# State products as 64 by 64 quarters, mask and decay tables by scans on chip, plan with later landings

## The chip, the cores and the metric

The kernel runs on one core of a Trainium2 chip. The metric is device time in microseconds (us), the median of several executions. TensorE is called PE here, VectorE DVE, ScalarE ACT, GpSimd POOL and SyncE SP; SP issues nearly all DMAs.

## What is computed

The reference is a linear attention with a decay for each of 8 heads, followed by two token-wise two-layer networks. Cut to what matters:

```python
# q, k, v: (2, 8, 768, 64); lam: 8 rates in 0.97 .. 0.99
Dmask = where(rel >= 0, lam ** rel, 0)                     # inside a block
intra = ((q_block @ k_block.T) * Dmask) @ v_block
inter = (q_block * lam ** (pos + 1)) @ kv_state            # what came before the block
kv_state = lam ** block * kv_state + (k_block * lam ** (block - 1 - pos)).T @ v_block
x = (intra + inter)                                        # 1536 tokens of 512 features
h = x @ w_in; x = (h * tanh(softplus(h))) @ w_out           # 512 -> 2048 -> 512
out = (relu(x @ w2_in) ** 2) @ w2_out
```

The kernel takes blocks ("chunks") of 128 positions, which gives the same result: 6 chunks in each of the 2 sequences, 12 in all.

## The kernel before

**Tiling.** A chunk `c` arrives as two tiles of 512 KB: `qk` (queries and keys, the 64 features of an even head on partitions 0 to 63, of the odd head on 64 to 127, four head pairs side by side) and `kv` (keys and values by position). `attention(j)` treats two chunks. For each chunk PE makes the scores `sc` (L392, 8 products), DVE multiplies them with `mask` into `a` (L271), PE multiplies `a` with the values into `xo` (L433, 8 products) and adds the state's part (L437, 8 products into the same bank). POOL scales the keys by the mask's last column (L398) and the queries by the decays `pw` (L403). PE makes the update `sd` of the state (L415), ACT or POOL scales the old state (L451, L447) and DVE adds the update (L271, or L462 for a sequence's first). The attention's output goes out of PSUM as `xh` (rounded) and `xl` (the rest), which the first network's `up` products read; its later tokens as `xr`.

**The state** is kept as 128 by 128 for each head pair, with the two heads' 64 by 64 blocks on the diagonal and zeros off it. Thus L437 contracts over 128 partitions, half of which are zeros, into 64 output columns. POOL zeroes the tile at L421; DVE adds each update in two instructions, one per head (64 partitions each).

**Tables.** The rates `lam` come by a tiny DMA on the ACT queue; seven DVE instructions (L324) double up the powers in eight rows; SP writes them to DRAM (`tab_d`, L338) and reads them back twice as `mask` (L344: row p starts p places earlier, 256 KB each) and twice as decays (L351).

**Weights** come as 64-bit numbers in tiles `st` of 512 KB; ACT and DVE make `m`, `t` and then the rounded `wh` and the rest `wl`. The networks' products are `up`, `p`, `b`, `e` and `dn`, all of 512 columns in three roundings (L278).

**Order.** `Plan` puts every operation in a list with an assumed length, and `plan.run(14.0, UNITS)` walks an assumed clock and picks, on each engine, the due operation whose inputs are ready. The order so found is fixed: engines then run their lists in order and wait on semaphores. `FIRST` fixes the order of SP's first DMAs, `LAG` is what is assumed between an operation's end and its effect. Ten products on zeros (L307) stand at the head of PE's list.

Of the kernel before, what the change touches and what calls it, by code (L numbers as in the profile page):

```python
# [20 lines left out]
P = 128  # L21
H = 8
# [35 lines left out]
class Plan:  # L58
# [7 lines left out]

    LAG = {"PE": 0.35, "DVE": 0.2, "ACT": 0.3, "POOL": 0.25, "SP": 2.2}

# [148 lines left out]
def attention_mlps(ctx, tc, lam, qk, kv, w_in, w_out, w2_in, w2_out, out):  # L217
# [19 lines left out]
    banks = ctx.enter_context(tc.tile_pool(name="banks", bufs=1, space=PSUM))  # L237
    dram = ctx.enter_context(tc.tile_pool(name="dram", bufs=1, space=bass.MemoryType.DRAM))
# [52 lines left out]

    W = 2 * CH
    tab_d = dram.tile([H, W], F32, name="tab_d")
    misc = Val("misc")
# [4 lines left out]

    def tab():  # L300
        return tl(misc, 4, W)[0:H, 2]

    def warm_up():

        z = zeros()
        for _ in range(WARM):
            nc.tensor.matmul(out=tl(warm)[:, 0], lhsT=z[:, 0:P], rhs=z, start=True, stop=True)  # L307

    warm = Val("warm", "P")
    zval = Val("zero", dtype=BF16)  # L310
    misc_parts = [(misc, "pw"), (misc, "tab")]

# [20 lines left out]

    op("ACT", 0.1, lambda: nc.scalar.dma_start(out=tab()[:, CH : CH + 1], in_=lam), [], [(misc, "lam")],
       name="lam", lag=2.2, due=0.0)
    op("DVE", 0.4, ones, [], [(misc, "tab")], name="ones")
    op("DVE", 1.2, powers, [(misc, "lam")], [(misc, "tab")], name="powers")
    op("SP", 0.1, lambda: nc.sync.dma_start(out=tab_d, in_=tab()), [(misc, "tab")], [("tab_d", 0)],  # L338
       name="tab_d", lag=2.2, due=FIRST["tab_d"])

    def masks():
        for e in range(2):

            nc.sync.dma_start(  # L344
                out=tl(mask, 2, NP, CH)[:, e],
                in_=bass.AP(tab_d.tensor, tab_d.offset + e * W, [[1, P], [2 * W, NP], [1, CH]]),
            )

    def decays():
        for e in range(2):  # L350
            nc.sync.dma_start(  # L351
                out=pw()[e * D : (e + 1) * D],
                in_=bass.AP(tab_d.tensor, tab_d.offset + e * W + CH, [[0, D], [2 * W, NP], [1, CH]]),
            )

    op("SP", 1.6, masks, [("tab_d", 0)], [(mask, 0)], name="masks", due=FIRST["masks"])
    op("SP", 0.9, decays, [("tab_d", 0)], [(misc, "pw")], name="decays", due=FIRST["decays"])


# [8 lines left out]
    def attention(j):  # L368
# [14 lines left out]
        for n, c in enumerate(cs):  # L383
            q, k, a = qks[n], kvs[n], avs[n]
            sc = Val(f"sc{c}", "P")

            def scores(sc=sc, q=q):
                t, o = tl(q, 2, NP, CH), tl(sc, 2, NP, CH)
                for p in range(NP):
                    for e in range(2):  # L390
                        r = slice(e * D, (e + 1) * D)
                        nc.tensor.matmul(out=o[:, e, p], lhsT=t[r, 1, p], rhs=t[r, 0, p], start=True, stop=True)  # L392

            op("PE", 0.95, scores, [(q, "q"), (q, "k")], [(sc, 0)], name=sc.name, rank=rank + n)
            op("DVE", 1.3, lambda a=a, sc=sc: tt(tl(a, 2, NP, CH), tl(sc, 2, NP, CH), tl(mask, 2, NP, CH), ALU.mult),
               [(sc, 0), (mask, 0)], [(a, 0)], name=a.name)
            if not (last and n):
                op("POOL", 1.3, lambda k=k: nc.gpsimd.tensor_tensor(  # L398
                    out=tl(k, NP, 4, D)[:, :, 1:3], in0=tl(k, NP, 4, D)[:, :, 1:3],
                    in1=tl(mask, 2, NP, CH)[:, :, :, CH - 1 : CH].rearrange("p e n o -> p n e o").to_broadcast(  # L400
                        [P, NP, 2, D]), op=ALU.mult), [(k, "k"), (mask, 0)], [(k, "k")], name=f"kd{c}")
            if not first or n:
                op("POOL", 1.35, lambda q=q: nc.gpsimd.tensor_tensor(  # L403
                    out=tl(q, 2, NP, CH)[:, 0], in0=tl(q, 2, NP, CH)[:, 0], in1=pw(), op=ALU.mult),
                   [(q, "q"), (misc, "pw")], [(q, "q")], name=f"qd{c}")
        sd, xo = Val(f"sd{j}", "P"), Val(f"xo{j}", "P")
# [12 lines left out]
        if first:  # L419
            state[s] = Val(f"state{s}")  # L420
            op("POOL", 1.1, lambda v=state[s]: nc.gpsimd.memset(tl(v), 0.0), [], halves(state[s]), name="state0")  # L421
        sv = state[s]
        for n, c in enumerate(cs):
            fresh = first and n == 0

            def outs(k=kvs[n], a=avs[n], q=qks[n], n=n, fresh=fresh, sv=sv):
                v, w, qd = tl(k, NP, 4, D), tl(a, 2, NP, CH), tl(q, 2, NP, CH)[:, 0]

                z, o = tl(sv, 2, NP, P)[:, n], tl(xo, NP, 2, CH)
                for p in range(NP):  # L430
                    for e in range(2):

                        nc.tensor.matmul(out=o[e * D : (e + 1) * D, p, n], lhsT=v[:, p, 0 if e else 3],  # L433
                                         rhs=w[:, e, p], start=True, stop=fresh)
                    for e in range(0 if fresh else 2):
                        r = slice(e * D, (e + 1) * D)
                        nc.tensor.matmul(out=o[r, p, n], lhsT=z[:, p, r], rhs=qd[:, p], start=False, stop=True)  # L437

            op("PE", 0.95 if fresh else 1.9, outs,
               [(kvs[n], "v"), (avs[n], 0)] + ([] if fresh else [(qks[n], "q"), (sv, n)]),  # L440
               [(xo, n)], name=f"xo{c}", rank=rank + 20 + n)
            if last and n:
                continue
            def scale(sv=sv, n=n):
                z, last = tl(sv, 2, NP, P), pw()[:, :, CH - 1 : CH]
                if t:
                    nc.gpsimd.tensor_tensor(  # L447
                        out=z[:, 1 - n], in0=z[:, n], in1=last.to_broadcast([P, NP, P]), op=ALU.mult)
                    return
# [3 lines left out]
            if not fresh:  # L453
                op("POOL" if t else "ACT", 1.3 if t else 1.2, scale, [(sv, n), (misc, "pw")], [(sv, 1 - n)],
                   name=f"ss{c}")

            def add(sv=sv, n=n, fresh=fresh):
                z, d = tl(sv, 2, NP, P)[:, 1 - n], tl(sd, 2, 2, NP, D)[:, 0, n]
                for e in range(2):
                    r = slice(e * D, (e + 1) * D)  # L460
                    if fresh:
                        nc.vector.tensor_copy(out=z[r, :, r], in_=d[r])  # L462
                    else:
                        tt(z[r, :, r], d[r], z[r, :, r], ALU.add)

            op("DVE", 0.9, add, [(sd, n), (sv, 1 - n)], [(sv, 1 - n)], name=f"sa{c}")
        cols = slice(i * 2 * CH, (i + 1) * 2 * CH)
        for p in range(2):
            if single(0, t):
                if i == 0:  # L470
                    x_hi[0, t, p], x_lo[0, t, p] = Val(f"xh{t}{p}", dtype=F32R), Val(f"xl{t}{p}", dtype=F32R)
                hi, lo = x_hi[0, t, p], x_lo[0, t, p]
                op("ACT", 0.65, lambda hi=hi, p=p: copy(tl(hi)[:, :, cols], tl(xo, 2, 2, 2 * CH)[:, p]),
                   [(xo, 0), (xo, 1)], [(hi, i)], name=hi.name)
                op("DVE", 0.75, lambda hi=hi, lo=lo, p=p: tt(
                    tl(lo)[:, :, cols], tl(xo, 2, 2, 2 * CH)[:, p], tl(hi)[:, :, cols].bitcast(F32), ALU.subtract),
                   [(xo, 0), (xo, 1), (hi, i)], [(lo, i)], name=lo.name)
            else:
# [9 lines left out]
    def weights(L, g, kind, kk):  # L488
# [4 lines left out]
        for i in range(2):  # L493
# [389 lines left out]
```

## Time and profile before

| | us |
|---|---|
| median of 3 runs (566.04 to 567.22) | 567.0 |
| the profiled execution: span from the first to the last instruction | 564.7 |
| PE busy in it | 549.6 |
| DVE, ACT, POOL busy | 307.6, 333.2, 33.1 |

The profiled execution has no time of its own beside its span. The median lies 2.3 us above that span; the difference is what surrounds the first and the last instruction, and it is taken as the same for both kernels. PE is busy in 97% of the span, so the time is PE's work plus the stretches at the start in which PE waits.

### The profile page before, as it was taken

The numbers are of one execution on the slowest core, as the hardware profiler recorded it, in microseconds if no ns is written. First come the engines' busy times: TensorE is split into PE (matmuls) and PEld (weight loads), VectorE is DVE, ScalarE is ACT, GpSimd is POOL, SyncE is SP. The second block draws the span as 40 slices with busy tenths as digits, with TensorE's granted clock in tenths as the row PEclk, the third lists the DMA queues.
The fourth block names the chain that finished last, engine by engine and source line by source line (L and its number), as shares of the span: only waits on it lengthen the run. The fifth ranks groups of instructions, "written<-read, shape, count | busy, mean of one in ns | idle before, by whom it ended". The sixth has DMA issues, their size and how long they took to land.

```text
span 564.7 us, 7047 instructions
## 1 busy us (share of the span) xinstructions
PE 549.6 (97%) x2934; PEld 454.9 (81%) x2934; DVE 307.6 (54%) x339; ACT 333.2 (59%) x374; POOL 33.1 (6%) x31
## 2 busy tenths in 40 slices
PE   3989999999999999999999999999999999999997
PEld 1878888888888888888888888888888888888885
DVE  2876985951453833582688865434363635743301
ACT  1435364643764566545886877347964789546920
POOL 1654600000000000000000000000000000000000
PEclk9899999999999999999999999999999999999999
DMA  8999000222141106041400401311222112300022
GB/s 238 409 409 339 6 2 0 75 74 74 38 149 38 38 2 203 21 122 65 149 1 0 150 0 38 111 39 37 76 74 75 60 48 79 113 0 1 18 95 111
DMA packets 15998, 50.52 MB, mean 89 GB/s; under 512 B 1624, under 2 KB 3168, under 8 KB 15968
## 3 DMA queue, kind: packets, MB, share of 16 engines
q1 hardware_dynamic: 15952, 50.08, 25.5%
q8 instruction: 23, 0.38, 0.3%
q14 instruction: 7, 0.06, 0.0%
q10 hardware_dynamic: 16, 0.00, 0.0%
HBM read 46.92 MB, written 3.15 MB: 89 GB/s over the span
## 4 chain that ended last, share of the span: by engine, by line
PE 96%; DMA 2%; DVE 1%; issue 0%; SPq 0%; DVEq 0%
PE dn L278 46%; PE up L278 20%; PE p L278 13%; PE e L278 7%; PE b L278 3%; PE xo L433 2%; PE sc L392 2%; PE xo L437 1%; DMA mask<-tab_d 1%; PE sd L415 1%; DVE t L510 0%; DMA tab_d<-misc 0%; DVE state L271 0%; DVE misc L324 0%; DMA misc<-in_lam_dram 0%
## 5 line engine op out<-in xcount | busy, mean ns | idle before, releaser
L515 DVE SCALAR_TENSOR_TENSOR t<-m,t 128x1024 int32<-128x1024 int32 x64 | 78.5, 1231 | 63.5 <-ACT m L507 61.4
L268 ACT ACTIVATE ac<-dn 128x1024 f32<-128x1024 f32 x46 | 47.3, 1029 | 101.9 <-PE dn L278 101.9
L271 DVE TENSOR_TENSOR gl<-h,gh 128x1024 fp32r<-128x1024 f32 x48 | 58.7, 1227 | 78.0 <-ACT gh L268 77.6
L278 PE MATMUL dn<-gh,wl 128*128 128x512 f32 x192 | 74.7, 389 | 0.0
L278 PE MATMUL dn<-wh,gh 128*128 128x512 f32 x192 | 74.7, 389 | 0.0
L278 PE MATMUL dn<-wh,gl 128*128 128x512 f32 x192 | 74.7, 389 | 0.0
L278 PE MATMUL dn<-gh,wh 128*128 128x512 f32 x192 | 74.7, 389 | 0.0
L278 PE MATMUL dn<-wl,gh 128*128 128x512 f32 x192 | 74.7, 389 | 0.0
L278 PE MATMUL dn<-gl,wh 128*128 128x512 f32 x192 | 74.7, 389 | 0.0
L268 ACT ACTIVATE gh<-h 128x1024 fp32r<-128x1024 f32 x48 | 50.3, 1053 | 0.7
L507 ACT ACTIVATE m<-st 128x512 f32<-128x512 f32 x64 | 40.1, 664 | 10.5 <-DMA st<-in_moe_w_in_dram 6.8
L271 DVE TENSOR_TENSOR wl<-t,wh 128x1024 fp32r<-128x1024 f32 x32 | 39.6, 1246 | 12.1 <-ACT wh L268 12.1
L606 ACT ACTIVATE h<-up 128x1024 f32<-128x1024 f32 x20 | 20.6, 1029 | 38.2 <-PE up L278 32.5
L268 ACT ACTIVATE wh<-t 128x1024 fp32r<-128x1024 f32 x32 | 33.4, 1052 | 15.3 <-DVE t L515 15.2
L278 PEld LDWEIGHTS dn<-gh,wl 128*128 128x128 f32 x192 | 36.0, 188 | 7.5
L278 PEld LDWEIGHTS dn<-wh,gh 128*128 128x128 f32 x192 | 36.0, 188 | 7.5
L278 PEld LDWEIGHTS dn<-gl,wh 128*128 128x128 f32 x192 | 36.0, 188 | 7.5
L278 PEld LDWEIGHTS dn<-wl,gh 128*128 128x128 f32 x192 | 36.0, 188 | 7.5
L278 PEld LDWEIGHTS dn<-wh,gl 128*128 128x128 f32 x192 | 36.0, 188 | 7.4
L278 PEld LDWEIGHTS dn<-gh,wh 128*128 128x128 f32 x192 | 36.0, 188 | 7.4
L268 ACT ACTIVATE dn<-ac 128x1024 f32<-128x1024 f32 x34 | 34.4, 1019 | 0.2
L510 DVE TENSOR_SCALAR t<-st 128x512 int32<-128x512 int32 x64 | 26.8, 446 | 7.0 <-DMA st<-in_moe_w_in_dram 5.7
(102 smaller groups left out, 987.3 us busy)
## 6 DMA issues: line engine op xcount, KB each, us to landing
st<-in_moe_w_in_dram SPq DMA_DIRECT2D x32, 512.0 KB, 4.7
st<-in_moe_w_out_dram SPq DMA_DIRECT2D x32, 512.0 KB, 3.6
qk<-in_qk_dram SPq DMA_DIRECT2D x12, 512.0 KB, 10.6
kv<-in_kv_dram SPq DMA_DIRECT2D x12, 512.0 KB, 10.4
out_dram<-ac SPq DMA_DIRECT2D x4, 512.0 KB, 2.8
out_dram<-ac SPq DMA_DIRECT2D x4, 256.0 KB, 2.0
mask<-tab_d SPq DMA_DIRECT2D x2, 256.0 KB, 6.3
misc<-tab_d SPq DMA_DIRECT2D x2, 128.0 KB, 6.8
```

What stands on the lines that cost most here:

```text
L268: nc.scalar.activation(out=o, in_=i, func=AF.Copy)
L271: nc.vector.tensor_tensor(out=o, in0=a, in1=b, op=alu)
L278: nc.tensor.matmul(out=out_, lhsT=a, rhs=b, start=first and i == 0 and not onto, stop=last and i == 2, skip_group_check=onto)
L392: nc.tensor.matmul(out=o[:, e, p], lhsT=t[r, 1, p], rhs=t[r, 0, p], start=True, stop=True)
L415: nc.tensor.matmul(out=o[e * D : (e + 1) * D, p], lhsT=t[:, p, 1 + e], rhs=t[:, p, 0 if e else 3], start=True, stop=True)
L433: nc.tensor.matmul(out=o[e * D : (e + 1) * D, p, n], lhsT=v[:, p, 0 if e else 3], rhs=w[:, e, p], start=True, stop=fresh)
L437: nc.tensor.matmul(out=o[r, p, n], lhsT=z[:, p, r], rhs=qd[:, p], start=False, stop=True)
L507: op("ACT", 0.67, lambda st=st, i=i: nc.scalar.activation(out=tl(m)[:, i], in_=tl(st, TB, 2)[:, :, 1].bitcast(F32), func=AF.Copy, scale=RA ...
L510: op("DVE", 0.5, lambda st=st, i=i: nc.vector.tensor_scalar(out=tl(t)[:, i], in0=tl(st, TB, 2)[:, :, 0], scalar1=29, scalar2=None, op0=ALU ...
L515: nc.vector.scalar_tensor_tensor(out=tl(t), in0=tl(m).bitcast(I32), scalar=scalar, in1=tl(t), op0=shift, op1=ALU.bitwise_or)
L606: op("ACT", 1.05, lambda: nc.scalar.activation(out=tl(h), in_=tl(src), func=AF.Relu if L else AF.Mish), halves(src), [(h, 0)], name=h.name)
```

## The change

1. **State free of zeros.** The state of a head pair is 128 by 64 (`tl(sv, 4, NP, D)`): the even head on partitions 0 to 63, the odd head on 64 to 127. The state's products are split from `outs` into `carried`: each contracts over 64 partitions into 64 columns, and four in a row take the four quarters of the array. For head pairs 2 and 3 the two heads change places in the output (`weighted`), and the tiles of the first network's `w_in` that meet them are loaded in two halves that change places too. The POOL memsets go; the scaling has half the elements; the addition is one DVE instruction instead of two, and for a sequence's first chunk an ACT copy.
2. **Tables on chip.** `tab_d`, its DMAs and the doubling go. `lam` is fetched as one row, PE spreads it over the partitions by three products of one row (`spread`, after three of the ten warm-up products), DVE copies that to SBUF, POOL writes an identity (`diagonal`), and DVE makes the eight masks and the four decays by one scan each.
3. **Plan.** SP's first DMAs are `qk0 kv0 st00000 ...`, the lag of SP's DMAs is 3.8 instead of 2.2, and the walk starts its due times at 6.0 instead of 14.0.

```diff
-    LAG = {"PE": 0.35, "DVE": 0.2, "ACT": 0.3, "POOL": 0.25, "SP": 2.2}
+    LAG = {"PE": 0.35, "DVE": 0.2, "ACT": 0.3, "POOL": 0.25, "SP": 3.8}
...
-        "st00000 qk0 tab_d kv0 st00001 masks decays qk1 kv1 qk2 kv2 qk3 kv3 st00010 st00011".split())}
+        "qk0 kv0 st00000 qk1 kv1 st00001 qk2 kv2 qk3 kv3 st00010 st00011".split())}
...
-    op("PE", 4.3, warm_up, [(zval, 0)], [(warm, 0)], name="warm", rank=-3000)
...
+    op("PE", 1.3, lambda: warm_up(3), [(zval, 0)], [(warm, 0)], name="warm", rank=-3000)
+
+    def spread():
+        o = tl(lamp)[:, 0]
+        nc.tensor.matmul(out=o[:, 0:H], lhsT=one(), rhs=row(), start=True, stop=True)
         for e in range(2):
...
+            nc.tensor.matmul(out=o[e * D : (e + 1) * D, H : H + NP], lhsT=one()[:, 0:D], rhs=row()[:, e::2],
+                             start=True, stop=True)
+
+    def diagonal():
+        nc.gpsimd.memset(tl(misc, 2, 4, CH)[:, 1, 0:2], 0.0)
+        nc.gpsimd.affine_select(out=eye(), in_=eye(), pattern=[[1, CH]], compare_op=ALU.not_equal, fill=1.0,
+                                base=1 - CH, channel_multiplier=1)
...
+    op("PE", 2.9, lambda: warm_up(WARM - 3), [(zval, 0)], [(warm, 0)], name="warm", rank=-2998)
...
+    def run_of_powers(out_, lam_, add, first):
+        nc.vector.tensor_tensor_scan(out=out_, data0=lam_.to_broadcast([P, CH]), data1=add, initial=first,
+                                     op0=ALU.mult, op1=ALU.add)
+
+    def masks(n):
+        for h in range(4 * n, 4 * n + 4):
+            run_of_powers(tl(mask, 2, NP, CH)[:, h % 2, h // 2], rate()[:, h : h + 1], eye(), 0.0)
...
-            op("POOL", 1.1, lambda v=state[s]: nc.gpsimd.memset(tl(v), 0.0), [], halves(state[s]), name="state0")
...
+            def carried(q=qks[n], n=n, sv=sv):
+                z, o, qd = tl(sv, 4, NP, D)[:, n], tl(xo, NP, 2, CH), tl(q, 2, NP, CH)[:, 0]
+                for p in range(2):
+                    for e in range(2):
+                        for h in (p, p + 2):
+                            r = slice(e * D, (e + 1) * D)
+                            nc.tensor.matmul(out=o[weighted(h, e), h, n], lhsT=z[r, h], rhs=qd[r, h], start=False,
+                                             stop=True, skip_group_check=True)
...
+                if fresh:
+                    copy(z, d)
+                else:
+                    tt(z, d, z, ALU.add)
...
+                if L == 0 and kind == 0 and k >= 2:
+
+                    for e in range(2):
+                        nc.sync.dma_start(out=tl(st, TB, 2)[e * D : (e + 1) * D], in_=ap[(1 - e) * D : (2 - e) * D])
+                    return
...
-    order = plan.run(14.0, UNITS)
+    order = plan.run(6.0, UNITS)
```

Below, a digit after a name is the chunk (`sc1`) or the pair of chunks (`xo0`, `sd0`); what follows the underscore is a buffer's number. On **DVE**, at the start of the list, before:

```order
L324 TENSOR_SCALAR misc_68<-misc_68 8x64
L510 TENSOR_SCALAR t0000_96<-st00000_72 128x512
L510 TENSOR_SCALAR t0000_96<-st00001_112 128x512
L271 TENSOR_TENSOR a0_123<-sc0_103,mask_114 128x1024
L515 SCALAR_TENSOR_TENSOR t0000_96<-m0000_98,t0000_96 128x1024 x2
L271 TENSOR_TENSOR a1_164<-sc1_142,mask_114 128x1024
L462 COPY state0_70<-sd0_154 64x4x64 x2
```

and in the changed kernel, where the scans print as SCALAR_TENSOR_TENSOR of 128 by 128:

```order
L346 COPY misc_65<-lamp_80 128x12
L351 SCALAR_TENSOR_TENSOR mask_94<-misc_65 128x128 x8
L351 SCALAR_TENSOR_TENSOR misc_65<-misc_65 128x128 x4
L270 TENSOR_TENSOR a0_123<-sc0_105,mask_94 128x1024
L533 TENSOR_SCALAR t0000_138<-st00000_92 128x512
L270 TENSOR_TENSOR a1_169<-sc1_157,mask_94 128x1024
L533 TENSOR_SCALAR t0000_138<-st00001_121 128x512
L538 SCALAR_TENSOR_TENSOR t0000_138<-m0000_125,t0000_138 128x1024
L270 TENSOR_TENSOR state0_149<-sd0_129,state0_149 128x256
```

Twelve scans now stand ahead of `a0`; the two instructions on the first weight tile come behind it, and `a1` no longer stands behind two long ones.

On **PE**, from the first scores on, before:

```order
L392 MATMUL sc0_103<-qk0_87 128x128 x8
L433 MATMUL xo0_133<-a0_123,kv0_101 64x128 x8
L392 MATMUL sc1_142<-qk1_121 128x128 x8
L415 MATMUL sd0_154<-kv0_101 64x64 x8
L392 MATMUL sc2_170<-qk2_131 128x128 x8
L415 MATMUL sd0_154<-kv1_126 64x64 x8
L433 MATMUL xo0_133<-a1_164,kv1_126 64x128 x2
L437 MATMUL xo0_133<-qk1_121,state0_70 64x128 x2
```

and now:

```order
L401 MATMUL sc0_105<-qk0_68 128x128 x8
L424 MATMUL sd0_129<-kv0_78 64x64 x8
L443 MATMUL xo0_140<-a0_123,kv0_78 64x128 x8
L401 MATMUL sc1_157<-qk1_99 128x128 x8
L424 MATMUL sd0_129<-kv1_114 64x64 x8
L443 MATMUL xo0_140<-a1_169,kv1_114 64x128 x8
L452 MATMUL xo0_140<-qk1_99,state0_149 64x128 x8
```

The state's products stood two by two between those of `a`; now they stand eight in a row behind them. Before, the scores of six chunks (0 to 4 and 6) precede the first `up`; now of five (0 to 4).

On **SP**, the first DMAs before:

```order
L502 DMA st00000_72<-in_moe_w_in_dram 128x1024
L379 DMA qk0_87<-in_qk_dram 128x1024
L338 DMA tab_d_63<-misc_68 8x256
L381 DMA kv0_101<-in_kv_dram 128x1024
L502 DMA st00001_112<-in_moe_w_in_dram 128x1024
L344 DMA mask_114<-tab_d_63 128x4x128 x2
L351 DMA misc_68<-tab_d_63 64x4x128 x2
L379 DMA qk1_121<-in_qk_dram 128x1024
```

and now:

```order
L388 DMA qk0_68<-in_qk_dram 128x1024
L390 DMA kv0_78<-in_kv_dram 128x1024
L525 DMA st00000_92<-in_moe_w_in_dram 128x1024
L388 DMA qk1_99<-in_qk_dram 128x1024
L390 DMA kv1_114<-in_kv_dram 128x1024
L525 DMA st00001_121<-in_moe_w_in_dram 128x1024
L388 DMA qk2_127<-in_qk_dram 128x1024
```

Five DMAs of tables are gone, and none of those left waits for a computation at this place.

## Rows read from the trace of the kernel before

**Rows 1.** The page: busy time of PE, share of the span, instructions.

```profile
PE 549.6 (97%) x2934; PEld 454.9 (81%) x2934; DVE 307.6 (54%) x339; ACT 333.2 (59%) x374; POOL 33.1 (6%) x31
```

**Rows 2.** Chain that ended last, in order of time: start us, us, what.

```profile
0.73 1.38 DMA misc<-in_lam_dram
...
3.92 1.78 DMA tab_d<-misc
...
6.15 6.75 DMA mask<-tab_d
...
13.03 1.23 DVE a L271
...
14.31 1.98 PE xo L433 x16
16.28 2.01 PE sc L392 x16
...
22.88 1.09 PE sc L392 x16
23.98 0.61 PE sd L415 x16
...
24.81 0.22 PE xo L437 x4
```

**Rows 3.** Busy time by stretch: stretch, length, engines (instructions), granted clock, DMA share, GB/s.

```profile
7.00:14.30 7.30, 0.53 (x10) 0.34 (x7) 1.70 (x3) 0.67 (x1) 1.24 (x2) 0.80 1.02 255
14.30:18.30 4.00, 3.99 (x34) 3.44 (x36) 2.31 (x2) 1.06 (x1) 1.77 (x2) 0.52 1.02 409
...
32.40:42.00 9.60, 9.55 (x52) 7.54 (x52) 6.96 (x6) 3.19 (x3) 5.57 (x5) 1.00 1.03 410
42.00:70.00 28.00, 27.73 (x426) 24.29 (x426) 21.17 (x28) 12.59 (x19) 15.05 (x11) 1.00 0.49 179
70.00:100.00 30.00, 30.00 (x149) 24.89 (x146) 22.05 (x25) 16.77 (x19) 0.00 (x0) 1.00 0.00 1
```

**Rows 4.** Timeline of PE: start, us, instruction [idle before it <-releaser].

```profile
1.19 3.96 PE L307 MATMUL warm<-zero 128*128 128x512 bf16 x10 [1.19 <-DVE zero L318]
...
33.08 0.50 PE L278 MATMUL up<-xl,wh 128*128 128x512 f32 x1
```

**Rows 5.** Timeline of POOL: its first two instructions of the kernel.

```profile
0.73 0.95 POOL L421 MEMSET state<- 128x1024 f32 x1 [0.29 <-POOLq L870]
13.06 1.06 POOL L398 TENSOR_TENSOR kv<-kv,mask 128x512 f32<-128x512 f32 x1 [11.38 <-DMA mask<-tab_d]
```

**Rows 6.** DMA queues between 1.7 and 24 us: packets, MB, share of 16 engines.

```profile
q1 hardware_dynamic: 3426, 7.41, 99.5%
q10 hardware_dynamic: 10, 0.00, 0.0%
```

**Rows 7.** Groups by shape, first 70 us: busy us, mean ns of one | idle before.

```profile
L271 DVE TENSOR_TENSOR state<-sd,state 64x256 f32<-64x256 f32 x16 | 6.7, 421 | 2.6 <-POOL state L447 1.9 <-PE sd L415 0.4
...
L324 DVE TENSOR_SCALAR misc<-misc 8x64 f32<-8x64 f32 x1 | 0.2, 242 | 0.0
```

**Rows 8.** Groups by shape, whole span.

```profile
L271 DVE TENSOR_TENSOR wl<-t,wh 128x1024 fp32r<-128x1024 f32 x32 | 39.6, 1246 | 12.1 <-ACT wh L268 12.1
...
L510 DVE TENSOR_SCALAR t<-st 128x512 int32<-128x512 int32 x64 | 26.8, 446 | 7.0 <-DMA st<-in_moe_w_in_dram 5.7 <-DMA st<-in_moe_w_out_dram 1.2
...
L271 DVE TENSOR_TENSOR a<-sc,mask 128x1024 f32<-128x1024 f32 x12 | 14.6, 1221 | 8.7 <-PE sc L392 5.9 <-DMA mask<-tab_d 2.5
```

**Rows 9.** Timeline of DVE between 12 and 34 us.

```profile
18.34 1.23 DVE L271 TENSOR_TENSOR a<-sc,mask 128x1024 f32<-128x1024 f32 x1 [1.70 <-PE sc L392]
...
27.76 2.33 DVE L510 TENSOR_SCALAR t<-st 128x512 int32<-128x512 int32 x2
...
32.33 0.69 DVE L271 TENSOR_TENSOR xl<-xo,xh 128x512 fp32r<-128x512 f32 x1
```

**Rows 10.** Busy time by stretch, the first 6 us (columns as rows 3).

```profile
0.00:6.00 6.00, 3.96 (x10) 1.29 (x10) 2.38 (x11) 1.95 (x2) 1.16 (x5) 1.00 0.62 196
```

More of the change, by code (lines that the diff above doesn't have):

```diff
@@ L298, in pw, with eye, none, one @@
         return tl(misc, 2, 4, CH)[:, 0]
-    def tab():
-        return tl(misc, 4, W)[0:H, 2]
-    def warm_up():
+    def eye():
+        return tl(misc, 8, CH)[:, 4]
+    def none():
+        return tl(misc, 8, CH)[:, 5]
+    def one():
+        return tl(misc, 8, CH)[0:1, 6]
+    def rate():
+        return tl(misc, 8, CH)[:, 7, 0 : H + NP]
+    def row():
+        return tl(misc, 8, CH)[0:1, 7, D : D + H]
+    def warm_up(n):
         z = zeros()
-        for _ in range(WARM):
+        for _ in range(n):
             nc.tensor.matmul(out=tl(warm)[:, 0], lhsT=z[:, 0:P], rhs=z, start=True, stop=True)
-    warm = Val("warm", "P")
+    warm, lamp = Val("warm", "P"), Val("lamp", "P")
     zval = Val("zero", dtype=BF16)
-    misc_parts = [(misc, "pw"), (misc, "tab")]
     def zeros():
@@ L334, in attention_mlps @@
[L334 to L341, printed above, removed]
-        for e in range(2):
[L344 to L347, printed above, removed]
@@ L349, in decays @@
-    def decays():
[L350 to L357, printed above, removed]
+    op("PE", 1.3, lambda: warm_up(3), [(zval, 0)], [(warm, 0)], name="warm", rank=-3000)
@@ new lines, in attention_mlps @@
+    op("ACT", 0.1, lambda: nc.scalar.dma_start(out=row(), in_=lam.rearrange("h o -> o h")),
+       [], [(misc, "row")], name="lam", lag=1.6, due=-9.0)
+    op("POOL", 0.2, lambda: nc.gpsimd.memset(one(), 1.0), [], [(misc, "one")], name="one", due=-10.0)
+    op("PE", 0.3, spread, [(misc, "row"), (misc, "one")], [(lamp, 0)], name="spread", rank=-2999)
+    op("PE", 2.9, lambda: warm_up(WARM - 3), [(zval, 0)], [(warm, 0)], name="warm", rank=-2998)
+    op("DVE", 0.2, lambda: nc.vector.tensor_copy(out=rate(), in_=tl(lamp)[:, 0, 0 : H + NP]), [(lamp, 0)],
+       [(misc, "lam")], name="rate", due=-8.5)
@@ new lines, in attention_mlps @@
+    op("POOL", 0.9, diagonal, [], [(misc, "eye")], name="eye", due=-9.0)
+    def run_of_powers(out_, lam_, add, first):
[4 more added lines that the diff above has]
+            run_of_powers(tl(mask, 2, NP, CH)[:, h % 2, h // 2], rate()[:, h : h + 1], eye(), 0.0)
+    def decays():
+        for p in range(NP):
+            run_of_powers(pw()[:, p], rate()[:, H + p : H + p + 1], none(), 1.0)
@@ L360, in attention_mlps @@
+    for n in range(2):
+        op("DVE", 1.3, lambda n=n: masks(n), [(misc, "lam"), (misc, "eye")], [(mask, n)], name=f"mask{n}", due=-8.0 + n)
+    op("DVE", 1.3, decays, [(misc, "lam"), (misc, "eye")], [(misc, "pw")], name="decay", due=2.0)
+    masked = [(mask, 0), (mask, 1)]
+    decayed = [(misc, "pw")]
     x_hi, x_lo, x_raw = {}, {}, {}
@@ L453, in attention @@
             if not fresh:
-                op("POOL" if t else "ACT", 1.3 if t else 1.2, scale, [(sv, n), (misc, "pw")], [(sv, 1 - n)],
-                   name=f"ss{c}")
+                op("POOL" if t else "ACT", 0.7 if t else 0.9, scale, [(sv, n), *decayed], [(sv, 1 - n)], name=f"ss{c}")
             def add(sv=sv, n=n, fresh=fresh):
[L458 to L466, printed above, removed]
+                z, d = tl(sv, 4, NP, D)[:, 1 - n], tl(sd, 2, 2, NP, D)[:, 0, n]
+                if fresh:
+                    copy(z, d)
+                else:
+                    tt(z, d, z, ALU.add)
+            op("ACT" if fresh else "DVE", 0.5, add, [(sd, n), *([] if fresh else [(sv, 1 - n)])], [(sv, 1 - n)],
+               name=f"sa{c}")
+        out_of = [key for key in plan.wrote if key[0] is xo]
         cols = slice(i * 2 * CH, (i + 1) * 2 * CH)
```

56 lines of the change are left out of this document (22 added, 34 removed).

## Prediction, made before the changed kernel was run

> **What bounds the kernel now.** I read the page first: PE is busy for 549.6 of 564.7 us [rows 1], so only two things can move the time, what PE does and when it waits. The table by stretch [rows 3] puts the waiting at the start: 0.53 us of PE work between 7 and 14.3 us, while from 70 us on PE has no gap. I then read the chain of waits in order of time [rows 2]. It is one line of table making: rates landed at 2.11, powers, `tab_d` written from 3.92 to 5.70, `mask` read back until 12.90, first `a` on DVE at 13.03, first `xo` on PE at 14.31. [...] After that DVE is the slow engine of the start: its last `xl` before the first network starts at 32.33 us and ends at 33.02, and PE's first product that reads `xl` starts at 33.08 [rows 4, 9]. From there on PE is the bound. So the sum has two terms: how much earlier that `xl` ends, and what PE has to do behind it.
>
> **When the tables are ready.** Rates: landed at 2.11 as before. PE has started three zero products by then, 0.40 us each (ten in 3.96 us, from 1.19 on) [rows 4], so `spread` starts at about 2.4. Its three products of one row are six records; at half clock a record of `sc` is 2.01/16 = 0.13 us [rows 2], so 0.2 to 0.75 us; I take 0.45, to 2.85. The DVE copy of twelve numbers is like the narrowest rows, 0.24 us [rows 7], with hand-overs 0.1: rates at 3.2. The identity on POOL: a zeroing of 1024 numbers a partition takes 0.95 us [rows 5], so 256 take 0.24 and the row of ones 0.1, from 0.73 to 1.1; the select over 128 numbers is bounded by 0.1 and by the 1.06 us of a two-input row of 512 [rows 5]; with 0.35 the identity stands at 1.5, under the cover of the rates. A rival below takes that cover away.
>
> The twelve scans have no row. The DVE row of 256 numbers takes 0.42 us, of 1024 1.22 [rows 7, 8], so 0.155 us fixed and 1.04 ns a number: 128 numbers at one a cycle are 0.29 us. A scan does two operations in which each number needs the one before; at two cycles it is the row of 256, 0.42. I take 0.42 and keep 0.29 for the range. 12 x 0.42 = 5.05: `a0` starts at 3.2 + 5.05 + 0.1 = **8.35** instead of 13.03. The decays, four of the twelve, stand ahead of `a0` and cost it 1.7 us of that; nothing else of this start waits for them.
>
> **From a0 to the first network.** Before, from 13.03 to 33.02 us. Now DVE has, up to the `xl` that counts, four `a` (4.88), four `t` (1.78), two joins of bits (2 x 1.23 as other rows of 1024), three state additions of one row of 256 (1.26), one `wl` (1.25) and three `xl` (2.07) [rows 7 to 9]: 13.7 us. Waits: behind `a0` PE does `xo` and `sc1`, at full clock 0.87 (four records of such a product are 0.22 [rows 2]) and 1.09, and 0.15 of hand-overs, less one `t` of 0.45 between: 1.7, what DVE waited there before, too [rows 9]. For the other hand-overs to ACT and PE 0.5. And DVE runs some instructions longer while POOL works: the two `t` at 27.76 took 2.33 us instead of 0.89 [rows 8, 9]; I take a third of that again, 0.5. In all 16.4, so `xl` ends at 8.35 + 16.4 = 24.75 instead of 33.02: **8.3 us** earlier.
>
> Data must keep up. Before, the first 6 us moved 196 GB/s, 1.18 MB [rows 10], and queued transfers then ran at 409 [rows 3], 1.28 us for a tile of 512 KB. Without the waits for `tab_d` the first six tiles are queued at once. The tenth tile (`kv3`) then lands near 6 + (5.24 - 1.18)/0.409 = 15.9 us, the thirteenth (`qk4`, whose scores stand ahead of the first `up`) at 19.8. Both are ahead of DVE, which reaches the last `a` of the four some 9.5 us after `a0`, near 18. The `w_in` tiles in two halves are 8 more issues, 0.3 to 0.4 us each on SP, which has long waits for buffers later: nothing.
>
> **PE's work behind it.** Seven chunks' state products (4, 5, 7 to 11) lie where PE is the bound; the three earlier ones hide under DVE. Now 16 records take 4 x 0.22 = 0.87 us [rows 2], two column halves at a time. Four quarters at a time would give 0.44. The nearest row with as small weights is `sd`, 16 records of 64 columns in 0.61 us [rows 2]; I take that, 0.26 less for each chunk, 1.8 in all, with 0.44 (3.0) and the 1.09 us of `sc`, whose products also contract over 64 (a loss of 1.5), as ends. Against it, one `sc` more stands behind the first `up` than before: 1.1 us. Net **0.7 us** earlier. The state's shorter additions and scalings are off the path there: DVE and POOL are busy 21 and 15 of 28 us from 42 to 70 [rows 3].
>
> **Sum.** 564.7 - 8.3 - 0.7 = 555.7 us of span, and with the 2.3 us between span and median **558.0**.
>
> **Rivals.** *POOL starts late.* The select is the first POOL instruction of the kernel that is not a memset. Before, the first such one ran at 13.06, right when its mask had landed, 11.38 us after the memset [rows 5]. So POOL may need anything from 0 to 11.4 us to get ready, and the trace hides it. For the forecast: a load of code would have to move bytes, and between 1.7 and 24 us only the queues of SP and ACT moved any [rows 6]. Against it: that profile need not list such a transfer. With half of the 11.4, 5.7 us, the identity stands at 7.15, `a0` at 7.25 + 5.05 = 12.3; PE idles as before and `xo` and `sc1` run at half clock, 2.0 us more; `xl` ends at 12.3 + 16.4 + 2.0 = 30.7, 2.3 earlier, and the time is 567.0 - 2.3 - 0.7 = **564.0**. [...]
>
> *POOL starts very late, and the kernel is slower.* The same at the upper bound, 11.4 us: identity at 12.85, `a0` at 18.0, `xl` at 36.4, 3.4 later, less 0.7: **569.7**. It is slower from a delay of 8.7 us on. Nothing but the missing row speaks for so much.
>
> *The quarters do not overlap.* The head as forecast, but 0.87 us or more for each chunk's state products: the 1.8 us are lost, **559.8**, and 561.3 at 1.09. For it: no row shows four quarters at once. Against it: both kinds of halves overlap in `sc` and `xo`. [...]
>
> *The change does not do what it says.* The start is bound by something else, say DMA tiles landing 5 us later than I work out: 562 to 565.
>
> **How the numbers follow.** Forecast 0.52, POOL late by some 6 us 0.26, quarters that do not overlap 0.12, POOL very late 0.05, otherwise bound 0.05. The forecast's own range is 558.0 - 1.5 (scans of 0.29) - 1.2 (quarters at full overlap) = 555.3 up to about 560. For 8 in 10 the range has to reach the case of a late POOL: **555.5 to 564.2**. About 0.2%, 1.1 us, is what a measurement of this kernel can tell from none. Faster by more than that, below 565.9: all but the very late POOL and a part of the last cases, 0.93; the same 0.03; slower 0.04.
>
> **What would show it.** Right: the first `a` near 8.4 us, scans of 0.42 us, the first `up` with `xl` near 24.8, no half clock on PE behind its first idle stretch, `in` groups of 16 records in about 0.6 us, and no wait of PE from there on. Wrong: a select on POOL that starts later than 2 us (then everything behind it moves with it), scans at 0.29 or above 0.5, state products at 0.87 or more, PE waiting for a `qk` or `kv` tile before the first `up`, or any new gap of PE behind 70 us, where the changed plan has put other instructions in other places.

## The result, and the profile of the changed kernel

The changed kernel takes **560.5 us** (median of four runs, 559.0 to 562.5) against 566.8 for the kernel before in the same session: ratio 0.989, 95% interval 0.986 to 0.991. The forecast was 558.0 (555.5 to 564.2): the direction and the range hold, but of the 9 us forecast about 6 came. The profiled execution has a span of 558.7 us and a time of 560.9.

PE's busy time answers [rows 1]; it is 1.3 us less than before. The next fences are the head: POOL's select, then DVE (start, us, instruction, [idle before it <-releaser]); they answer [rows 5, 9]. The last of them gives the durations of single scans (shortest, median and longest in ns, then first and last start).

```profile
PE 548.3 (98%) x2940; PEld 451.5 (81%) x2940; DVE 303.6 (54%) x331; ACT 332.4 (59%) x376; POOL 32.0 (6%) x32
```

```profile
1.25 0.29 POOL L338 TENSOR_SCALAR_AFFINE_SELECT misc<-misc 128x128 f32<-128x128 f32 x1
```

```profile
3.52 0.17 DVE L346 COPY misc<-lamp 128x12 f32<-128x12 f32 x1 [2.39 <-PE lamp L333]
3.80 2.63 DVE L351 TENSOR_TENSOR_SCAN mask<-misc 128x128 f32<-128x128 f32 x8
6.35 2.16 DVE L351 TENSOR_TENSOR_SCAN misc<-misc 128x128 f32<-128x128 f32 x4
8.44 1.19 DVE L270 TENSOR_TENSOR a<-sc,mask 128x1024 f32<-128x1024 f32 x1
...
11.92 1.23 DVE L270 TENSOR_TENSOR a<-sc,mask 128x1024 f32<-128x1024 f32 x1 [1.96 <-PE sc L401]
...
21.52 0.42 DVE L270 TENSOR_TENSOR state<-sd,state 128x256 f32<-128x256 f32 x1 [1.21 <-PE sd L424]
...
23.87 0.43 DVE L533 TENSOR_SCALAR t<-st 128x512 int32<-128x512 int32 x1 [0.46 <-DMA st<-in_moe_w_in_dram]
25.51 0.42 DVE L270 TENSOR_TENSOR state<-sd,state 128x256 f32<-128x256 f32 x1 [1.22 <-ACT state L469]
26.48 0.69 DVE L270 TENSOR_TENSOR xl<-xo,xh 128x512 fp32r<-128x512 f32 x1 [0.54 <-ACT xh L267]
```

```profile
L351 DVE TENSOR_TENSOR_SCAN mask<-misc x8: 397/398/424, 3.8 to 6.0; 128x128 f32<-128x128 f32 x8
L351 DVE TENSOR_TENSOR_SCAN misc<-misc x4: 394/396/1218, 6.4 to 8.1; 128x128 f32<-128x128 f32 x4
```

The first `a` starts at 8.44 us (13.03 before, [rows 2]). The `xl` that counts ends at 26.48 + 0.69 = 27.17, not at 24.75: behind `a0` DVE idles five times, 5.39 us in all, where 2.2 were forecast. The last two of these waits lead to ACT, whose timeline shows what it stood for:

```profile
21.58 0.70 ACT L530 ACTIVATE m<-st 128x512 f32<-128x512 f32 x1 [3.64 <-DMA st<-in_moe_w_in_dram]
23.86 0.67 ACT L530 ACTIVATE m<-st 128x512 f32<-128x512 f32 x1 [1.58 <-DMA st<-in_moe_w_in_dram]
24.43 1.05 ACT L469 ACTIVATE state<-state,misc 128x64 f32<-128x64 f32 x4
25.39 1.06 ACT L267 ACTIVATE xh<-xo 128x512 fp32r<-128x512 f32 x2
```

ACT waits 3.64 and 1.58 us for the two `w_in` tiles that come in halves. Behind these conversions, in the order the plan gave ACT, stand the scaling of the state (L469) and the `xh` that the first network needs. PE (answering [rows 4]) waits for the same queue:

```profile
20.72 0.69 PE L424 MATMUL sd<-kv 128*64 128x64 f32 x16 [0.99 <-POOL kv L407]
...
24.84 2.08 PE L401 MATMUL sc<-qk 64*128 64x128 f32 x16 [1.97 <-DMA qk<-in_qk_dram]
26.85 0.79 PE L277 MATMUL up<-xh,wh 128*128 128x512 f32 x1
27.45 0.63 PE L277 MATMUL up<-xh,wl 128*128 128x512 f32 x1
27.87 0.56 PE L277 MATMUL up<-xl,wh 128*128 128x512 f32 x1
...
73.39 0.39 PE L277 MATMUL dn<-gl,wh 128*128 128x512 f32 x1
```

`qk4` is there only at 24.8 us. The scores that waited for it take 2.08 us, like those of 2.01 us in [rows 2] at a granted clock of 0.52 [rows 3], and the second `up` product 0.63 where later ones take 0.39. The table by stretch (columns as [rows 3]) shows it as a granted clock of 0.60, and beside it the transfers' low rate in the stretches ahead, 303 GB/s:

```profile
14.30:18.30 4.00, 3.45 (x68) 3.02 (x70) 4.00 (x5) 2.98 (x7) 3.38 (x2) 1.00 1.06 303
18.30:24.00 5.70, 3.58 (x80) 2.76 (x76) 4.03 (x7) 0.84 (x2) 2.29 (x2) 1.00 1.01 303
24.00:28.00 4.00, 3.16 (x19) 2.74 (x20) 2.25 (x4) 2.44 (x7) 1.88 (x2) 0.60 1.03 410
```

So the first product with `xl` starts at 27.87 instead of 33.08, 5.2 us earlier, and the first `dn` at 73.39 instead of 79.41, 6.0 earlier. The `dn` of before:

```profile
79.41 0.39 PE L278 MATMUL dn<-gl,wh 128*128 128x512 f32 x1
```

From there to the end both kernels take 485.3 us.

### The profile page after: what moved, and what is told of

Same layout as the page of the kernel before. It is cut to its first block, busy times and chain, and to the rows that moved or that the text cites. A ratio compares the mean times of both kernels' runs of the same rounds, so it can differ in the third digit from the quotient of the medians.

```text
span 558.7 us, 7060 instructions
## 1 busy us (share of the span) xinstructions
PE 548.3 (98%) x2940; PEld 451.5 (81%) x2940; DVE 303.6 (54%) x331; ACT 332.4 (59%) x376; POOL 32.0 (6%) x32
## 4 chain that ended last, share of the span: by engine, by line
PE 95%; DMA 4%; SPq 0%; issue 0%; DVE 0%
PE dn L277 47%; PE up L277 20%; PE p L277 14%; PE e L277 7%; DMA qk<-in_qk_dram 4%; PE b L277 3%; PE sc L401 2%; PE xo L443 1%; PE xo L452 1%; PE sd L424 1%; SPq L390 0%; SPq L525 0%; SPq L388 0%; DVE ac L270 0%
## 5 line engine op out<-in xcount | busy, mean ns | idle before, releaser
L533 DVE TENSOR_SCALAR t<-st 128x512 int32<-128x512 int32 x64 | 25.4, 422 | 4.9 <-PE dn L277 4.2
```

What stands on the lines that cost most here:

```text
L533: op("DVE", 0.5, lambda st=st, i=i: nc.vector.tensor_scalar(out=tl(t)[:, i], in0=tl(st, TB, 2)[:, :, 0], scalar1=29, scalar2=None, op0=ALU ...
```

## The experiments

**Theory:** the four transfers that bring `st00010` and `st00011` in halves (L523), which the forecast put at nothing, are slow, and ACT, DVE, POOL and PE wait for them or for what is queued behind them. **Rival:** DVE's own work was put too low, and the waits only fill the time. The kernel before was timed beside each group of runs: 566.7, 566.7, 567.0 and 566.7 us.

### Whole tiles, heads swapped in the input layout

```diff
-                if L == 0 and kind == 0 and k >= 2:
-                    for e in range(2):
-                        nc.sync.dma_start(out=tl(st, TB, 2)[e * D : (e + 1) * D], in_=ap[(1 - e) * D : (2 - e) * D])
-                    return
...
-        return a.reshape(B, NP, 2, nch, CH, Dd).transpose(0, 3, 1, 2, 4, 5).reshape(B * nch, NP, 2, CH, Dd)
+        a = a.reshape(B, NP, 2, nch, CH, Dd).transpose(0, 3, 1, 2, 4, 5).reshape(B * nch, NP, 2, CH, Dd)
+        return np.concatenate([a[:, :2], a[:, 2:, ::-1]], axis=1)
+    lam = np.concatenate([lam.reshape(NP, 2)[:2], lam.reshape(NP, 2)[2:, ::-1]])
```

> The changed kernel, but the heads of pairs 2 and 3 are swapped where the inputs are laid out, so the features come out in order and every w_in tile is one whole transfer of 128 partitions again; instructions and their order on all engines are those of the changed kernel. Theory (the half tiles are what the forecast left out: they land at 21.5 and 23.8 us, and two ACT conversions that wait for them stand ahead of the state scaling and the xh that the first network needs, and qk4 lands behind them at 24.8): the tiles land by about 19.5 and qk4 by 21, ACT waits under 1 us for them, PE does not wait for qk4, the first product that reads xl starts near 25.2 instead of 27.87, and the time is 558.0 (557.3 to 558.7). Rival 1 (the half tiles cost nothing, DVE's own work was costed too low): the xl still ends at 27 and the time stays at 560.5. Rival 2 (PE then waits longer for DVE and falls to the lower clock all the same): data early, but the first products at half clock; 559 to 559.5.

**557.0 us** (556.9 to 557.3), ratio to before 0.983 (0.9815 to 0.9846). The instructions on PE, DVE, ACT and POOL are the changed kernel's, in its order. The timeline of ACT, DVE and PE, and two stretches of the table:

```profile
19.31 0.70 ACT L530 ACTIVATE m<-st 128x512 f32<-128x512 f32 x1 [1.13 <-DMA st<-in_moe_w_in_dram]
20.59 0.68 ACT L530 ACTIVATE m<-st 128x512 f32<-128x512 f32 x1 [0.58 <-DMA st<-in_moe_w_in_dram]
...
23.48 0.69 DVE L270 TENSOR_TENSOR xl<-xo,xh 128x512 fp32r<-128x512 f32 x1 [0.22 <-ACT xh L267]
...
22.23 1.16 PE L401 MATMUL sc<-qk 64*128 64x128 f32 x16
23.32 0.50 PE L277 MATMUL up<-xh,wh 128*128 128x512 f32 x1
...
24.23 0.50 PE L277 MATMUL up<-xl,wh 128*128 128x512 f32 x1 [0.18 <-DVE xl L270]
```

```profile
18.30:24.00 5.70, 5.68 (x98) 4.35 (x98) 5.33 (x9) 3.42 (x8) 3.00 (x3) 1.00 1.03 408
24.00:28.00 4.00, 3.82 (x18) 3.12 (x18) 3.97 (x4) 0.40 (x1) 4.00 (x3) 1.00 1.02 408
```

The transfers run at 408 GB/s, ACT stands 1.7 us for the two tiles instead of 5.2, PE does not wait for `qk4` (it lands at 21.8 us instead of 24.8), the granted clock stays at 1.00, `xl` ends at 24.17 and the first product with it starts 3.6 us earlier than in the changed kernel. The theory holds, with 0.3 us more gain than its range had, and the wait of PE for `xl` is 0.18 us: both rivals fall. `kv3` stands ahead of the halves in the queue and still lands earlier here, at 18.0 us instead of 19.5: the halves held tiles ahead of them, too.

### What is slow in a half tile

Two transfers for a tile again, on the layout of the run above, cut in two other ways: by columns, and by even and odd partitions.

```diff
+                        r = slice(e * TB // 2, (e + 1) * TB // 2)
+                        nc.sync.dma_start(out=tl(st, TB, 2)[:, r], in_=ap[:, r])
```

> The kernel with the heads swapped in the input layout, but the same w_in tiles go in two transfers again, now of 128 partitions and half the columns each. As many issues and bytes as the changed kernel has. Theory (a transfer that touches 64 partitions is what is slow): these run near 400 GB/s, qk4 lands near 21, time as with whole tiles, 558. Rival (the number of transfers, or two into one tile, is what is slow): 220 to 250 GB/s between 16 and 21 us, qk4 near 24.8, time 560.5.

```diff
+                        nc.sync.dma_start(out=tl(st, TB, 2)[e::2], in_=ap[e::2])
```

> The kernel with the heads swapped in the input layout, but the same w_in tiles in two transfers of 64 partitions each, the even and the odd ones instead of the lower and the upper. Theory 1 (what is slow is that all writes go to one half of the partitions): near 400 GB/s, qk4 lands near 21, time 557.0. Theory 2 (64 partitions are slow wherever they lie): 220 to 250 GB/s, qk4 near 24.8, time 560.5.

**556.9** (556.7 to 557.2) and **556.8** (556.6 to 557.3). The transfers between 16 and 21 us, first of the changed kernel, then of even and odd partitions (packets and rate; then queue, packets, MB, share of 16 engines):

```profile
DMA packets 349, 1.16 MB, mean 233 GB/s; under 512 B 65, under 2 KB 65, under 8 KB 349
q1 hardware_dynamic: 349, 1.16, 103.9%
```

```profile
DMA packets 596, 2.06 MB, mean 412 GB/s; under 512 B 93, under 2 KB 93, under 8 KB 596
q1 hardware_dynamic: 596, 2.06, 103.3%
```

In both, the 16 engines are busy all the time (103.9 and 103.3%), but each packet takes longer in the first: busy time over packets is 0.24 us against 0.14, for 3.3 and 3.5 KB. Neither the number of transfers nor that of their partitions costs anything here; where they go to 64 neighbouring partitions it is 233 GB/s instead of 412. One thing changes along with it: such a half also reads 64 neighbouring rows of the weights, where the other two cuts read half of each row or every second row. No run takes the two sides apart.

The 233 GB/s are those of a stretch that also holds the rest of `kv3`, a whole tile. At that rate the two tiles, 1.05 MB, would take an estimated 1.9 us longer than at the 408 GB/s of the run with whole tiles. In the trace `qk4`, the next tile behind them, lands 3.0 us later than there.

### Both halves at once

```diff
+                    for e, eng in enumerate((nc.sync, nc.sync if g else nc.scalar)):
+                        eng.dma_start(out=tl(st, TB, 2)[e * D : (e + 1) * D], in_=ap[(1 - e) * D : (2 - e) * D])
```

> The changed kernel with the swap, but of the first weights' two tiles the second half transfer of each goes out on ACT's queue, so that transfers to both halves of the partitions can run side by side. Theory 1 (one half of the partitions takes no more than 220 to 250 GB/s, two halves together the full rate): the two tiles land by about 20.5, qk4 by 21.5, time 557 to 558. Theory 2 (a transfer of 64 partitions is slow in itself): landings as in the changed kernel, 560.5. [...]

**563.2** (560.5 to 565.6), slower than either theory gave. The transfers between 16 and 18 us:

```profile
DMA packets 145, 0.48 MB, mean 242 GB/s; under 512 B 27, under 2 KB 27, under 8 KB 145
q1 hardware_dynamic: 80, 0.27, 54.3%
q10 hardware_dynamic: 65, 0.22, 45.1%
```

The engines do work for both queues there, and still move 242 GB/s. ACT issued its two halves (0.53 and 0.47 us) only at 11.97 and 14.96 us, behind a conversion and an `xh`, so the second tile was complete at 24.5. Whether the two queues' packets of that stretch went to different halves of the partitions, the trace doesn't show: inconclusive for the question, and a loss of 2.6 us against the changed kernel.

### Same data, another order

Two runs keep the half tiles and change who waits for them.

```diff
-            op("SP", 1.3, load, [], [(st, 0)], name=st.name, due=FIRST.get(st.name), spare=SPARE[0])
+            op("SP", 1.3, load, [], [(st, 0)], name=st.name, due=FIRST.get(st.name), spare=SPARE[0], lag=8.0 if name == "0001" else None)
```

> The changed kernel, with the landing of the two half-tile loads of the first weights put 4.2 us later in the plan alone: the transfers stay as they are, on ACT the two conversions move behind the state scaling and behind the first xh, and on DVE the two shifts move behind the state addition; later places of the plan shift a little too. Theory: ACT no longer stands 3.6 and 1.6 us for the half tiles, the xl that counts ends near 25 instead of 27.17; but the scores of qk4, which lands at 24.8, stand ahead of the first up on PE, so up starts near 26.9 as before and reads xl at about 27.4; time 560.0 (559.6 to 560.5). Rival (the ACT order is all, the wait for qk4 hides behind something): 558.

**560.6** (560.5 to 561.2), 0.1 above the expected range and far from the rival's 558. ACT without its long wait for tiles, and PE:

```profile
21.31 1.06 ACT L469 ACTIVATE state<-state,misc 128x64 f32<-128x64 f32 x4 [3.39 <-DVE state L270]
...
24.34 1.66 PE L401 MATMUL sc<-qk 64*128 64x128 f32 x16 [2.13 <-DMA qk<-in_qk_dram]
...
26.95 0.63 PE L277 MATMUL up<-xl,wh 128*128 128x512 f32 x1
```

The state's scaling comes 3.1 us earlier, the first product with `xl` 0.9, and no time is won: PE still waits 2.13 us for `qk4`, and then its scores take 1.66 us and the `up` product 0.63, against 1.16 and 0.50 in the run with whole tiles. The late tiles hold the start by two ways at once; to free ACT alone is worth nothing.

```diff
-        "qk0 kv0 st00000 qk1 kv1 st00001 qk2 kv2 qk3 kv3 st00010 st00011".split())}
+        "qk0 kv0 st00000 qk1 kv1 st00001 qk2 kv2 qk3 kv3 qk4 kv4 st00010 st00011".split())}
```

> The changed kernel with its half tiles, but qk4 and kv4 are queued ahead of st00010 and st00011; with that the plan puts the two ACT conversions behind the state scaling and the first xh, and the scores of qk4 ahead of av3. Theory: qk4 lands at about 18 to 19 and no engine on the way to the first up waits for the half tiles; the first product that reads xl starts near 25, the half tiles land near 24 to 27, early enough for the second half of the weights (needed near 33); time 558.0 to 558.7. Rival (the half tiles slow everything around them, whatever the order): kv3 and qk4 are late as before, 560.5.

**563.6** (561.7 to 567.0), a miss for both. DVE and ACT, in an execution of 566.1:

```profile
27.45 0.43 DVE L533 TENSOR_SCALAR t<-st 128x512 int32<-128x512 int32 x1 [4.15 <-DMA st<-in_moe_w_in_dram]
...
27.43 0.67 ACT L530 ACTIVATE m<-st 128x512 f32<-128x512 f32 x1 [4.17 <-DMA st<-in_moe_w_in_dram]
```

The plan had left one shift on DVE ahead of the state's addition and one conversion on ACT ahead of `xh`. The tile they need was now two places further back and landed at 27.4, so both engines stood 4.2 us. The expectation had counted the other conversions on ACT and not this one. Its landings were wrong, too: `qk4`, now ahead of the halves, landed at 22.2 us and not at 18 to 19, since the queue moved 222 GB/s from 18.3 to 24 us. `kv3`, `qk4` and `kv4` landed at 19.8, 22.2 and 24.6, some 2.4 us for each whole tile where the run with whole tiles takes 1.3. So this part of the rival held: the halves slow the tiles around them, those queued ahead of them as well.

### Half tiles in the kernel before

```diff
+                if L == 0 and kind == 0 and k >= 2:
+                    for e in range(2):
+                        nc.sync.dma_start(out=tl(st, TB, 2)[e * D : (e + 1) * D], in_=ap[e * D : (e + 1) * D])
+                    return
```

> The kernel before, with the w_in tiles of the first layer's second row pair brought in two transfers of 64 partitions each, each half to its own place (no swap). Theory (64 partitions are slow, but what that costs depends on who waits): these transfers run at 210 to 250 GB/s instead of 410 here too, so qk4 and the tiles behind them land some 3 to 4 us later; the kernel before starts its first network only at 33 us and has that much room, so the time stays within 0.2% of 566.7. Rival (the slow transfers cost their 3.5 us anywhere): 569 to 570.

**570.5** (569.4 to 571.3), ratio 1.006 (1.0038 to 1.0083): the theory of room fell. PE:

```profile
30.26 2.08 PE L392 MATMUL sc<-qk 64*128 64x128 f32 x16 [3.29 <-DMA qk<-in_qk_dram]
```

There too PE waits for a `qk` tile queued behind the halves, and the first product with `xl` moves from 33.08 to 36.80. The half tiles cost 3.8 us there and 3.5 in the changed kernel.

### Two quarters instead of four

With the head's slot always written to its own column half, the features come out in order and the tiles are whole.

```diff
-                c = e if p < 2 else 1 - e
+                c = e
...
-                    for e in range(2):
-                        for h in (p, p + 2):
+                    for h in (p, p + 2):
+                        for e in range(2):
```

> The changed kernel with head slot e always written to column half e, so that the state products use only the two quarters on the diagonal, the two taken in turn; the features then come out in order and the w_in tiles are whole transfers. Beside the run with the heads swapped in the input layout (557.0, sixteen records of a chunk's state products in 0.60 us) it has everything alike but the quarters. Theory of the forecast (four quarters give 0.26 us a chunk against two halves): 0.87 us or more a chunk, 1.8 to 2.5 us over seven chunks, 558.9 to 559.6. Rival (the gain is the smaller weights, not four quarters): 0.60 us again, 557.0.

**560.5** (560.3 to 560.6), a little above the theory's range. One chunk's state products here, then in the run with whole tiles and four quarters:

```profile
47.20 1.09 PE L452 MATMUL xo<-qk,state 64*64 64x128 f32 x16
48.22 2.06 PE L401 MATMUL sc<-qk 64*128 64x128 f32 x32
```

```profile
45.64 0.67 PE L452 MATMUL xo<-qk,state 64*64 64x128 f32 x16
46.24 2.06 PE L401 MATMUL sc<-qk 64*128 64x128 f32 x32
```

From one group's start to the next one's it is 1.02 against 0.60 us. Seven chunks make 2.9 us, and PE's stretch from the first product with `xl` to the first `dn` is 48.3 against 45.3. Two quarters are worse than the 0.87 us of the form with zero blocks: the smaller state pays on PE only because four quarters run side by side. And 560.5 is what the changed kernel takes, too: the half tiles cost what the four quarters bring.

### Is the start bound by DVE once the tiles are whole?

On the layout of the first run, the mask scans run twice.

```diff
-        for h in range(4 * n, 4 * n + 4):
+        for h in [*range(4 * n, 4 * n + 4)] * 2:
```

> The kernel with the heads swapped in the input layout (557.0), with the eight mask scans run twice: 8 x 0.33 = 2.6 us more of DVE ahead of the first a. Theory (with whole tiles the start is bound by DVE, as the forecast had it): a0 at 11.1 and everything to the first product that reads xl 2.0 to 2.6 us later, 559.0 to 559.7. Rival (the landings bind it, DVE has room): under 1 us later, 557.0 to 558.0.

**562.0** (562.0 to 562.1), above both ranges: 5.0 us more for 2.5 us of scans. PE:

```profile
12.21 1.97 PE L443 MATMUL xo<-a,kv 128*64 128x128 f32 x16 [0.93 <-DVE a L270]
14.11 2.08 PE L401 MATMUL sc<-qk 64*128 64x128 f32 x16
...
28.45 0.50 PE L277 MATMUL up<-xl,wh 128*128 128x512 f32 x1 [0.18 <-DVE xl L270]
```

The delay reaches the first network in full, and more: PE waits 2.38 and 0.93 us, and then `xo` and `sc` take 1.97 and 2.08 us instead of 1.09 and 1.16, with a granted clock of 0.72 from 7 to 14.3 us and 0.65 from there to 18.3 (1.00 in both with the scans once). That adds 1.8; with a longer wait for the second `wl`, 0.5 more, the first `dn` comes 4.7 later.

Two runs on the decay scans, which stand ahead of `a0`. Giving them a later due time left every instruction where it was:

> The kernel with the heads swapped in the input layout (557.0), with the four decay scans (2.16 us) given a later due time in the plan, so that they should stand behind a0 and fill DVE's idle 1.96 us there instead of standing ahead of a0. Theory (DVE bound up to the first network): a0 waits for sc0, which ends at 7.7, so it starts some 0.7 earlier at best and the first product that reads xl up to 0.7 earlier: 556.3 to 557.0. Rival (the decays are then late for the state scaling on ACT and for the scaled queries on POOL, which stand at 9.1 and 12.1): 557.5 to 558.5. If the plan puts them where they were, 557.0.

**557.4** (556.9 to 561.7), so it is a repeat of the first run and shows what medians of repeats differ by, 0.4 us; one of its six executions took 561.7. An order laid down does move them:

```diff
+    plan.follow(named["a0"], named["decay"])
```

> The kernel with the heads swapped in the input layout (557.0), with an order laid down in the plan that puts the four decay scans behind a0 on DVE; on PE the plan then puts the first state update behind the first inner products. Theory (DVE has idle time between a0 and a1 that can hold the decays): a0 starts at 7.75 instead of 8.43; PE's sd, now between the first inner products and the second scores, takes 0.6 of that back, so the first product that reads xl is 0.1 to 0.7 earlier, 556.3 to 557.0. Rival (pw comes too late for the state scaling on ACT, which stood at 9.1, and the scaled queries on POOL at 12.1): 557.5 to 558.5.

**557.5** (556.9 to 560.2): no gain. DVE:

```profile
7.70 1.23 DVE L270 TENSOR_TENSOR a<-sc,mask 128x1024 f32<-128x1024 f32 x1 [1.26 <-PE sc L401]
8.85 1.36 DVE L351 TENSOR_TENSOR_SCAN misc<-misc 128x128 f32<-128x128 f32 x4
...
11.68 1.22 DVE L270 TENSOR_TENSOR a<-sc,mask 128x1024 f32<-128x1024 f32 x1 [1.16 <-PE sc L401]
```

`a0` starts 0.73 earlier, `a1` only 0.24, and the first product with `xl` 0.08.

### The plan's numbers

On the layout of the first run, with the numbers of before.

```diff
-    LAG = {"PE": 0.35, "DVE": 0.2, "ACT": 0.3, "POOL": 0.25, "SP": 3.8}
+    LAG = {"PE": 0.35, "DVE": 0.2, "ACT": 0.3, "POOL": 0.25, "SP": 2.2}
-    order = plan.run(6.0, UNITS)
+    order = plan.run(14.0, UNITS)
```

> The kernel with the heads swapped in the input layout (557.0), with the plan's numbers put back to those of before: start 14 instead of 6 us and 2.2 instead of 3.8 us from a transfer's end to its use. On PE the first inner products then stand behind the second chunk's scores, and on DVE and ACT the conversions of later weights change places with gl and sl. Theory (the plan's numbers move what is off the path): 556.5 to 557.5. Rival (they carry a part of the gain): 558 or more.

**557.4** (556.9 to 557.7): the plan's two numbers are worth 0.4 us at most, which is what repeats differ by.

## Why the prediction was right, and where it was not

**When the tables are ready: right, by three misses that cancel; that the sum came out is luck.** The rates stood at 3.69 us, not 3.2: PE took 0.90 us for `spread` instead of 0.45. A scan took 0.40 us, near the forecast's 0.42, but the sum added durations, and in a row the scans start every 0.32 us, each before the one ahead of it has ended: the eight of the mask are done in 2.63 us. For twelve that is 1.2 us less. Against it, one of the four decay scans took 1.22 us while POOL scaled a tile of keys, 0.8 more than the others, which the sum had not counted there. From the first scan to `a0` it was 4.64 instead of 5.05, and `a0` started at 8.44 (forecast 8.35). The identity stood at 1.54 (forecast 1.5).

**POOL late, or very late: both fell.** The select ran at 1.25 us for 0.29, right behind the memset; the 11.38 us of idle in [rows 5] hid no delay. No run shows a delay of some 6 us, the rival's term.

**From a0 to the first network: right in its work, wrong in its waits.** From `a0` to the end of the `xl` that counts it was 18.7 us, not 16.4. With whole tiles it is 15.7, of which 2.3 are waits, as forecast. The 3.0 us between are waits, gone when the tiles are whole. Of the 8.85 us by which the first product with `xl` is then earlier than before, 4.6 lie ahead of `a0` and 4.3 behind it. No run makes only the tables or only the state, so how the 4.3 divide between them is not shown.

**"Data must keep up" is the step that failed.** It took 1.28 us for every 512 KB, at the 409 GB/s of [rows 3], and put the halves at "nothing" because it counted only their issue on SP. The rows of 409 and 410 GB/s hold whole tiles on 128 partitions. The one row of [rows 3] in which tiles go to 64 neighbouring partitions, the two transfers of decays, is that of 7 to 14.3 us, at 255 GB/s; the masks' short packets are mixed into it, so it gives no price, but it should have given the step a bound. At 233 GB/s `qk4` came at 24.8 and not 19.8, and the half tiles came when ACT's order, made for landings at 18.1 and 19.4 us in the plan, had long reached them. The price is 3.5 us: 560.5 against 557.0. Even whole tiles were later than the sum: in the first run PE waits for `qk3` until 16.30, where the sum has the ninth tile at 14.6, and `qk4` lands 2.0 us later than summed. The queue was not at 409 GB/s all the time: between 4.5 and 6.75 us it moved 229 to 273 GB/s in that run, and between 5 and 7 us 236 in the changed kernel, with whole tiles alone; why, no run shows.

**The rival "otherwise bound"** named just this, tiles 5 us later, at 562 to 565 and with a chance of 0.05. It was what happened, in part: most of the gain in the head (5.2 of 8.3 us) stayed, since `xl` was late anyway by DVE's own work.

**"No half clock behind the first idle stretch" was wrong for the profiled execution.** Behind the wait of 1.97 us for `qk4` PE ran at a granted clock of 0.50 from 24.8 to 28.0 us (1.00 from 18.3 to 24.8). It does not do so each time: of the four executions two show a mean granted clock of 1.000, at 560.2 and 559.0 us, and two 0.996 and 0.997, at 560.9 and 562.5. So the half clock is a part of the 3.5 us, and the late tiles cost time without it, too. "No wait of PE from there on" held but for 0.4 us at 52.9.

**PE's work behind it: right.** First product with `xl` to first `dn`: 46.33 us before, 45.52 after, 0.8 less (forecast 0.7). The state products take 0.60 us a chunk (forecast 0.61). The rival of quarters that do not overlap fell: 0.60 is less than the 0.87 of two at a time, and more than the 0.44 that the forecast estimated for four; what holds it there no run shows.

**The sum.** 8.3 + 0.7 = 9.0 us of span forecast; with whole tiles 8.85 + 1.1 = 9.9 (554.8), with the half tiles 5.2 + 0.8 = 6.0 (558.7). The mechanism was right, and one term that the sum put at zero was 3.5; that the sum for the start of `a0` held was in part luck, as said above.

## What to carry to other kernels

Cost a split transfer by how it is cut and not by how many parts it has: two halves by columns or by even and odd partitions cost nothing here (556.9 and 556.8 us against 557.0), two halves of 64 neighbouring partitions nearly halved the queue's rate (233 against 412 GB/s). When a head start is forecast, list with it every instruction that stands ahead of the critical one in each engine's program order and which transfer it waits for; a late tile that the critical work doesn't need held it through ACT's order. The rearrangement that made PE cheaper was free here in the layout of the inputs (557.0 us) and dear in a transfer (560.5). And add up a row of short instructions by the distance of their starts, not by their durations: 0.32 against 0.40 us for a scan here.

## What the runs showed of the hardware that was not expected

- Transfers into 64 neighbouring partitions: 233 GB/s with all 16 engines busy; into 64 even or odd ones 412. Whole tiles queued just ahead of such halves landed 2.4 us apart instead of 1.3.
- Sixteen records of 64 by 64 products: 0.60 us on four quarters, 1.02 on the two of the diagonal.
- A scan over 128 numbers takes 0.40 us, and scans in a row start every 0.32 us. Four took 2.16 us where POOL scaled a tile of keys beside them (6.52 to 7.60 us), because one of them, begun at 6.67, took 1.22 us; they took 1.36 where they stood behind that scaling.
- In the profiled executions PE's granted clock fell to 0.50 behind the wait of 1.97 us for `qk4` in the changed kernel; behind the waits of the run with whole tiles, the longest 1.34 us, it stayed at 1.00.
